# Router logits computed in two halves of 64 tokens, and the value products moved directly behind the next tile's scores

## The chip, the cores and the metric

The kernel runs on one NeuronCore of a Trainium2 chip. The metric is the device time of one execution in microseconds (us). A core has a matrix engine (TensorE; PE in the profile, its weight loads apart as PEld) and engines for elementwise work: VectorE (DVE), ScalarE (ACT) and GpSimd (POOL). SyncE (SP) issues most of the DMA transfers. Each engine takes its instructions in the order of the program, and the engines wait for each other by semaphores.

## The reference

Three layers in a row, cut to what matters:

```python
scores = (q @ k.T) / sqrt(64)                 # 4 batches, 8 heads, 576 positions, head size 64
scores = where((rel >= 0) & (rel < 64), scores, -1e9)   # causal window of 64 keys
attn   = exp(scores - max); attn /= attn.sum() + 1e-9
x      = (attn @ v)                           # as 2304 tokens x 512
noisy  = x @ w_gate + log1p(exp(x @ w_noise)) * noise   # router logits, 8 experts
# the top 2 experts of each token, softmax of their logits
x      = sum over the 2 experts of w * (relu(x @ w1[e]) @ w2[e])
out    = gate(x @ moe2_w_in) @ moe2_w_out     # dense feed-forward layer, hidden size 2048
```

## The kernel before, in words

The 2304 tokens are cut into 18 tiles of 128. The first 104 us are attention and routing, in which this change lies; then come the experts and the dense layer, about 845 us in which TensorE multiplies nearly without a pause.

The attention part is written out by hand as a loop over half-tile **steps** `u` (`step`, L676): a tile has an even step and an odd step. Each engine's queue has the order in which this code calls its parts:

- `A` (L347), in an even step: scores of the next tile. First four products that put the mask into two PSUM banks (L355, 64 rows by 64 columns of the array each), then 16 score products (L364) of the same shape. One bank holds the even heads of the tile, which are scores `u+2`, the other the odd heads, scores `u+3`. Three banks take turns, so the second bank that `A` writes is the one in which the even heads of the tile before stood.
- `Ex` (L418), in an even step: four transposes (L422) of an earlier tile's attention output; ScalarE copies the result to `xt` (L424).
- `C` (L383), in every step: four transposes (L387) of the softmax of one half; ScalarE copies them to `pt` (L389).
- `top` (L368) takes the row maxima on VectorE (L371) and their scaled negative on GpSimd (L373); `soft` (L376) is four exponentials on ScalarE (L380). `soft(u+2)` is called in step `u`.
- `Dm` (L392), at the end of an even step: 16 products with the values (L401, 128 rows by 64 columns of the array), and then the normalization on VectorE (L406, L407, L409) and the store of the tile.
- `Gm` (L435), in an odd step: the router logits of a tile whose `xt` is ready: four products of 128 by 128 (L440), copied out by VectorE (L443).
- `place` (L628): products that count tokens into slots (L634), from step 26 on; `advance` (L636): the routing's work on VectorE in small portions, and its products at L558 to L562.

`Ex`, `C` and `Gm` write two PSUM banks (`bank[3]`, `bank[5]`) in turn (`rot`, L335): within one tile `Ex` has the first, the even `C` the second, the odd `C` the first again, the logits the second. So the odd `C` can start when ScalarE has copied `xt` out. ScalarE's order in a tile is `xt`, even `pt`, exponentials of `u+2`, odd `pt`, exponentials of `u+3`; in every other tile two halves of a weight's conversion (L158) stand behind the exponentials.

Of the kernel before, what the change touches and what calls it, by code (L numbers as in the profile page):

```python
# [26 lines left out]
E, F = 8, 1024  # L27
# [30 lines left out]
def fused_kernel(ctx, tc, qT, kT, v, wg, noise, wcat, out, wd=None):  # L58
    nc = tc.nc
# [41 lines left out]
    def load_qk(j):  # L101
        q_t[j] = qbuf[:, j % 2]
        kt = k_t[j] = qk.tile([P, 4, 320], F32, tag="k", name=f"k{j}")

        for h in (slice(0, P), slice(P, 256)) if j == 0 else (slice(0, 256),):
            t = slice(256 * j + h.start, 256 * j + h.stop)
            nc.sync.dma_start(out=kt[:, :, 64 + h.start:64 + h.stop], in_=kTv[:, :, t])
            nc.sync.dma_start(out=q_t[j][:, :, h], in_=qTv[:, :, t])
        if j == 0:
            nc.vector.memset(kt[:, :, 0:64], 0.0)  # L110


    def keys_before(j):
        nc.gpsimd.tensor_copy(k_t[j][:, :, 0:64], k_t[j - 1][:, :, 256:320])
# [4 lines left out]
    def load_v(i):  # L119
        a = vp.tile([P, H * VW], F32, tag="vE", name=f"vE{i}")  # L120
        nc.sync.dma_start(out=a, in_=v[P * i:P * i + P, :])
        if i == 0:
            vO[0] = vp.tile([P, H * VW], F32, tag="vE", name="vE_")
            nc.vector.memset(vO[0][64:128, :], 0.0)
            nc.sync.dma_start(out=vO[0][0:64, :], in_=v[0:64, :])
        vE[i] = a
# [6 lines left out]
    def load_raw(n, eng=nc.sync):  # L133
        raws[n] = t = raw.tile([P, 1024], F32, tag="raw", name=f"raw{n}")
        if NF <= n < N2:

            if n % NF == 0:
                r = E - 2 if n >= NCE else (n // NF - 1) % (E - 2)
                dyn[n // NF] = nc.values_load(cnt_i[0:1, 1 + r:2 + r], engines=[mybir.EngineType.SP], min_val=0,
                                          max_val=(E - 1) * NF)  # L140
            eng.dma_start(out=t, in_=wcat[bass.ds(dyn[n // NF] + n % NF, 1)].rearrange("o p n -> (o p) n"))
        else:
            eng.dma_start(out=t, in_=wcat[n])
# [114 lines left out]
    wg_sb = ac.tile([P, 4, 32], F32, name="wg_sb")  # L258
# [76 lines left out]
    def rot(u):  # L335
        turn[0] += 1
        return bank[3 + 2 * (turn[0] % 2)] if u <= NU else bank[6]
# [9 lines left out]
    def A(i):  # L347
        j = i // 2
        qo, ko = (i % 2) * P, (i % 2) * P
        sb = [score(2 * i + k) for k in range(2)]  # L350
        for k in range(2):
            r = slice(64 * k, 64 * k + 64)
            for c in range(2):
                m = masks[c][int((2 * i + c) % 9 == 0)]
                nc.tensor.matmul(sb[k][64 * c:64 * c + 64, :], lhsT=id64[r, :],  # L355
                                 rhs=m[r].unsqueeze(1).to_broadcast([64, 4, P]), start=True, stop=False)
        for g in range(4):
            for c in range(2):
                for k in range(2):
                    r = slice(64 * k, 64 * k + 64)  # L360
                    keys = k_t[j][r, g, ko + 64 * c:ko + 64 * c + P]
                    if c == 0:
                        keys = keys.rearrange("p (s n) -> p s n", s=2)[:, ::-1, :]
                    nc.tensor.matmul(sb[k][64 * c:64 * c + 64, g * P:g * P + P],  # L364
                                     lhsT=q_t[j][r, g, qo + 64 * c:qo + 64 * c + 64],
                                     rhs=keys, start=False, stop=(g == 3))
# [9 lines left out]
    def soft(u):  # L376
        sb, nb = score(u), mxs.pop(u)
        p = wk.tile([P, 4, P], F32, tag="p", name=f"p{u}", bufs=4)
        for g in range(4):
            nc.scalar.activation(p[:, g, :], sb[:, g * P:g * P + P], AF.Exp, bias=nb[:, g:g + 1], scale=0.125)  # L380
        pr[u] = p

    def C(u):  # L383
        p = pr.pop(u)
        PTb = rot(u)
        for g in range(4):
            nc.tensor.transpose(PTb[:, g * P:g * P + P], p[:, g, :], idn)  # L387
        t = wk.tile([P, 512], F32, tag="pt", name=f"pt{u}", bufs=PTB)
        nc.scalar.activation(t, PTb, AF.Copy)  # L389
        pts[u] = t  # L390

    def Dm(u):  # L392
        i, r = divmod(u, 2)
        if r == 0:
            return
        ts = [pts.pop(2 * i + k) for k in range(2)]
        for h in range(H):
            g, k = divmod(h, 2)
            for c in range(2):
                vv = (vO, vE)[c][i]  # L400
                nc.tensor.matmul(OB[64 * c:64 * c + 64, h // 4, (h % 4) * VW:(h % 4) * VW + VW],  # L401
                                 lhsT=ts[k][:, g * P + 64 * c:g * P + 64 * c + 64], rhs=vv[:, h * VW:h * VW + VW],
                                 start=True, stop=True)
        ov = OB[:, :, 0:4 * VW].rearrange("p b (h d) -> p b h d", d=VW)
        rl = wk.tile([P, 2, 4, 1], F32, tag="rl", name=f"rl{i}")
        nc.vector.tensor_scalar(out=rl, in0=ov[:, :, :, D:VW], scalar1=1e-9, scalar2=None, op0=ALU.add)  # L406
        nc.vector.reciprocal(out=rl, in_=rl)  # L407
        x = wk.tile([P, H, D], F32, tag="x", name=f"x{i}", bufs=3)
        nc.vector.tensor_tensor(out=x.rearrange("p (b h) d -> p b h d", b=2), in0=ov[:, :, :, 0:D],  # L409
                                in1=rl.to_broadcast([P, 2, 4, D]), op=ALU.mult)  # L410
        xs[i] = x
        nc.sync.dma_start(out=x_dram[P * i:P * i + P, :], in_=x.rearrange("p h d -> p (h d)"))
        if i + 1 < NT:
            if i + 2 < NT:
                nc.gpsimd.tensor_copy(vE[i][0:64, :], vE[i + 1][0:64, :])
            vO[i + 1] = vE[i]
# [18 lines left out]
    def Gm(i, u):  # L435
        g, t = tile_group[i]
        xt = xts.pop(i)
        lg = (rot(u) if u <= NU else bank[0])[:, LGO:LGO + 2 * E]
        for k in range(4):
            nc.tensor.matmul(lg, lhsT=xt[:, k, :], rhs=wg_sb[:, k, 0:2 * E], start=(k == 0), stop=(k == 3))  # L440
        if t == 0:
            lgs_g[g] = gp.tile([P, max(GROUPS), 2 * E], F32, tag="lgs", name=f"lgs{g}", bufs=3)
        nc.vector.tensor_copy(lgs_g[g][:, t, :], lg)  # L443
# [184 lines left out]
    def place():  # L628
        while pq:
            c, o, ej = pq.popleft()  # L630
            if nids[0] == n_early:
                open_ids()
            nids[0] += 1
            nc.tensor.matmul(IDS2[:, c, :], lhsT=o, rhs=ej, start=False, stop=(nids[0] in (n_early, 2 * NT)))  # L634
# [23 lines left out]
    def open_ids():  # L658
        nc.tensor.matmul(IDS[:, 0:2 * NK], lhsT=wz[:, 0:P], rhs=wz[:, 0:2 * NK], start=True, stop=False)
# [16 lines left out]
    def step(u):  # L676
        for c in range(EW):
            if u == L0 + LS * c:
                load_raw(c)
        if u + 2 < NU:  # L680
            if (u + 2) % 4 == 0 and (u + 2) // 4 + 1 < NT // 2:
                load_qk((u + 2) // 4 + 1)
                keys_before((u + 2) // 4 + 1)
            if (u + 1) % 2 == 0 and (u + 1) // 2 + 1 < NT:
                load_v((u + 1) // 2 + 1)


        m = u // 2
        if u % 2 == 0:
            if u + 2 < NU:  # L690
                A(m + 1)
            if u == NU:
                nc.scalar.activation(vE[NT - 2][0:64, :], vE[NT - 1][0:64, :], AF.Copy)
            if u == NU - 2:
                C(u)
            if 0 <= m - 2 < NT:
                Ex(m - 2, u)
        if u < NU and u != NU - 2:
            C(u)
        if u % 2 == 0 and u + 2 < NU:  # L700
            top(u + 2)
            top(u + 3)
        if u + 2 < NU:
            soft(u + 2)

        if u % 2 == 1 and 0 <= m - 2 < NT:
            logits(m - 2, u)
        place()
        early()
        advance(MARKS[u > NU - 10])  # L710
        if 0 <= u - 1 < NU:
            Dm(u - 1)

        for c in range(EW):
            for h in range(2):
                if u == L0 + LS * c + 3 + h:
                    split_w(c, h)
                if u == L0 + LS * c + 4 + h and c < EW - 2:
                    rest_w(c, slice(512 * h, 512 * h + 512))
            if u == L0 + LS * c + 4 and EW <= c + 2 < NF:  # L720
                load_raw(c + 2)
# [291 lines left out]
    t0 = 0  # L1013
# [402 lines left out]
    for q, (ui, p) in enumerate(items):  # L1416
# [5 lines left out]
        while ndone < len(items) and ndone <= q + (1 if items[ndone][0] == FIRST2 else 2):  # L1422
            i = items[ndone]
# [84 lines left out]
```

## Time and profile before

| | |
|---|---|
| time, median of 3 runs | 947.45 us (947.38 to 947.93) |
| the profiled execution | 950.02 us, its span 948.3 us |
| busy over the span | PE 935.7 us (99%), DVE 665.6 (70%), ACT 436.5 (46%), POOL 186.2 (20%) |
| granted TensorE clock | 1.0 in the whole span |

A busy share over the whole span says little of the first tenth of it, which has limits of its own, so the rows below are read from that part. In a timeline a row merges instructions of one line that follow each other: start, time from the first's start to the last's end, engine, line, what is written from what, how many, and in brackets how long the engine stood idle before and what released it. A product of 32-bit numbers shows as two records, so 16 products are x32. Matmuls are pipelined: the ends that are shown overlap the next starts, so costs are read from start to start.

### The profile page before, as it was taken

To read this page: it belongs to the slowest core of one execution; us is meant where nothing else is said; L and a number is where in the kernel's file an instruction comes from. 1 tells how busy PE (TensorE), PEld (TensorE's weight loads), DVE (VectorE), ACT (ScalarE), POOL (GpSimd) and SP (SyncE) were. 2 spreads that over 40 slices of the span, in tenths; PEclk is the share of its full clock that TensorE was granted. 3 is DMA by queue.
4 is the path that set the end of the run, shared out by engine and by line. 5 is a ranking of instruction groups with operands and counts; after the bars stand their busy time and mean duration, and the time that the engine had idled before them with its cause. 6 is when DMAs were issued, how large, how long until landed. Compare 5 with 4: busy or idle time off the path is not lost. (4 is left out here: it accounts for less than half of the span.)

```text
span 948.3 us, 17990 instructions
## 1 busy us (share of the span) xinstructions
PE 935.7 (99%) x6779; PEld 832.3 (88%) x6781; DVE 665.6 (70%) x1411; ACT 436.5 (46%) x907; POOL 186.2 (20%) x249
## 2 busy tenths in 40 slices
PE   9999999999999999999999999999999999999998
PEld 6887888988888989898888889988999899899986
DVE  4689765477997968889533366767867776687664
ACT  6898314345565555555433266333433333342221
POOL 3222013133645353354402030000000000000000
PEclk9999999999999999999999999999999999999999
DMA  8874136555888878767725566775576559556521
GB/s 258 300 252 167 56 100 186 188 191 199 290 288 275 261 236 277 257 206 260 252 89 184 204 231 236 252 256 178 177 256 213 164 174 308 175 178 213 182 95 44
DMA packets 91274, 196.95 MB, mean 208 GB/s; under 512 B 7320, under 2 KB 18072, under 8 KB 91184
## 3 DMA queue, kind: packets, MB, share of 16 engines
q1 hardware_dynamic: 83152, 171.68, 54.6%
q0 software_dynamic: 6736, 21.86, 6.4%
q10 hardware_dynamic: 1296, 2.23, 0.6%
q8 instruction: 54, 0.88, 0.4%
q14 instruction: 36, 0.29, 0.1%
HBM read 155.45 MB, written 40.29 MB: 206 GB/s over the span
## 5 line engine op out<-in xcount | busy, mean ns | idle before, releaser
L969 PE MATMUL bank<-wo,hall 128*128 128x512 f32 x864 | 237.6, 394 | 0.0
L969 PE MATMUL bank<-w,hall 128*128 128x512 f32 (+3 forms) x944 | 234.6, 396 | 0.1
L969 PEld LDWEIGHTS bank<-w,hall 128*128 128x128 f32 (+3 forms) x944 | 167.7, 183 | 35.2 <-issue 0.3
L969 PEld LDWEIGHTS bank<-wo,hall 128*128 128x128 f32 x864 | 146.7, 188 | 17.4 <-DVE hall L915 0.2
L904 ACT ACTIVATE hall<-bank 128x288 fp32r<-128x288 f32 (+6 forms) x128 | 54.0, 422 | 218.4 <-PE bank L896 200.6
L896 PE MATMUL bank<-xhie,w 128*128 128x288 f32 (+4 forms) x768 | 122.5, 302 | 0.3 <-DVE hall L907 0.2
L896 PEld LDWEIGHTS bank<-xhie,w 128*128 128x128 f32 x768 | 113.5, 188 | 7.1 <-DVE hall L907 1.4
L907 DVE SCALAR_TENSOR_TENSOR hall<-bank,hall 128x288 fp32r<-128x288 f32 (+7 forms) x168 | 60.0, 391 | 82.5 <-ACT hall L904 75.1
L149 DVE TENSOR_TENSOR w<-raw,w 128x1024 fp32r<-128x1024 f32 (+1 forms) x69 | 81.9, 1188 | 23.8 <-ACT w L158 17.8
L1183 PEld LDWEIGHTS bank<-xb,wi 128*128 128x128 f32 x576 | 80.8, 188 | 8.4 <-DVE cg L1173 0.7
L1207 ACT ACTIVATE hall<-cg 128x512 fp32r<-128x512 f32 x64 | 40.3, 629 | 100.4 <-DVE cg L1205 100.4
L1183 PE MATMUL bank<-xb,wi 128*128 128x256 f32 x576 | 84.3, 282 | 0.3 <-DVE cg L1173 0.3
L1183 PEld LDWEIGHTS bank<-xc,wi 128*128 128x128 f32 x480 | 67.5, 188 | 6.5
L1183 PE MATMUL bank<-xc,wi 128*128 128x256 f32 x480 | 69.9, 280 | 0.0
L158 ACT ACTIVATE w<-raw 128x1024 fp32r<-128x1024 f32 (+1 forms) x71 | 69.4, 977 | 0.0
L896 PE MATMUL bank<-xloe,w 128*128 128x288 f32 (+4 forms) x384 | 69.0, 301 | 0.0
L1201 ACT ACTIVATE mg<-cg 128x512 f32<-128x512 f32 x64 | 40.1, 626 | 45.8 <-DVE cg L1173 44.1
L204 POOL TENSOR_TENSOR td<-rawd 128x512 f32<-128x512 f32 x32 | 33.3, 1040 | 139.6 <-DVE rawd L202 111.8
L896 PEld LDWEIGHTS bank<-xloe,w 128*128 128x128 f32 x384 | 58.0, 188 | 0.0
L1202 DVE SCALAR_TENSOR_TENSOR cg<-mg,cg 128x512 f32<-128x512 f32 x64 | 43.8, 684 | 18.8 <-ACT mg L1201 18.8
L1211 DVE SCALAR_TENSOR_TENSOR hall<-cg,hall 128x512 fp32r<-128x512 f32 x64 | 44.0, 687 | 8.1 <-ACT hall L1207 7.7
L1205 DVE SCALAR_TENSOR_TENSOR cg<-mg,cg 128x512 f32<-128x512 f32 x64 | 44.0, 687 | 1.0
(285 smaller groups left out, 1389.2 us busy)
## 6 DMA issues: line engine op xcount, KB each, us to landing
wi<-w1o SPq DMA_DIRECT2D x56, 1024.0 KB
raw<-wcat SPq DMA_DIRECT2D x64, 512.0 KB
rawd<-wd SPq DMA_DIRECT2D x32, 512.0 KB
w1o<-so SPq DMA_DIRECT2D x64, 256.0 KB
y<-y_dram SPq DMA_DIRECT2D x28, 256.0 KB
vE<-v SPq DMA_DIRECT2D x18, 260.0 KB
x_dram<-x SPq DMA_DIRECT2D x18, 256.0 KB
k<-kT SPq DMA_DIRECT2D x8, 512.0 KB
```

Of the source, the lines that this page charges most:

```text
L149: nc.vector.tensor_tensor(out=w[:, 1, c], in0=t[:, c], in1=w[:, 0, c].bitcast(F32), op=ALU.subtract)
L158: nc.scalar.activation(w[:, 0, c], t[:, c], AF.Copy)
L896: nc.tensor.matmul(ps, lhsT=l[k], rhs=r[:, k, s:s + w], start=(c == 0), stop=(c == len(prods) - 1))
L904: nc.scalar.activation(hh, ps, AF.Relu)
L907: nc.vector.scalar_tensor_tensor(out=t, in0=ps[:, c], scalar=0.0, in1=hh[:, c].bitcast(F32), op0=ALU.max, op1=ALU.subtract)
L969: nc.tensor.matmul(M2[b][0:w], lhsT=h2[:, o:o + w], rhs=r[n], start=(first and a == 0), stop=(last and a == end))
L1183: nc.tensor.matmul(ps, lhsT=w[:, l, k * P:k * P + P], rhs=r[:, m, k, :], start=(c == 0), stop=(c == len(prods) - 1))
L1201: nc.scalar.activation(st["m"], c, AF.Relu, scale=0.5)
L1202: nc.vector.scalar_tensor_tensor(out=c, in0=st["m"], scalar=1.0, in1=c, op0=ALU.min, op1=ALU.subtract)
L1205: nc.vector.scalar_tensor_tensor(out=c, in0=st["m"], scalar=1.0, in1=c, op0=ALU.min, op1=ALU.mult)
L1207: nc.scalar.activation(h2[:, 0:T], c, AF.Copy, scale=-1.0)
L1211: nc.vector.scalar_tensor_tensor(out=h2[:, T:2 * T], in0=c, scalar=-1.0, in1=h2[:, 0:T].bitcast(F32), op0=ALU.mult, op1=ALU.subtract)
```

## The change

Three edits. The router logits are computed by halves of 64 tokens: eight products of 128 rows by 64 columns of the array instead of four of 128 by 128, alternating between the two halves. `place` is called ahead of the logits instead of behind them. `Dm` keeps only its products and is called directly behind `A`, from step 4 on; the normalization becomes `norm` and is called where `Dm` was.

```diff
+    def norm(u):
+        i, r = divmod(u, 2)
+        if r == 0:
+            return
         ov = OB[:, :, 0:4 * VW].rearrange("p b (h d) -> p b h d", d=VW)
...
         for k in range(4):
-            nc.tensor.matmul(lg, lhsT=xt[:, k, :], rhs=wg_sb[:, k, 0:2 * E], start=(k == 0), stop=(k == 3))
+            for t0 in (0, 64):
+                s = slice(t0, t0 + 64)
+                nc.tensor.matmul(lg[s], lhsT=xt[:, k, s], rhs=wg_sb[:, k, 0:2 * E], start=(k == 0), stop=(k == 3))
...
                 A(m + 1)
             if u == NU:
                 nc.scalar.activation(vE[NT - 2][0:64, :], vE[NT - 1][0:64, :], AF.Copy)
+            if u > 2:
+                Dm(u - 1)
...
+        place()
         if u % 2 == 1 and 0 <= m - 2 < NT:
             logits(m - 2, u)
-        place()
         early()
         advance(MARKS[u > NU - 10])
         if 0 <= u - 1 < NU:
-            Dm(u - 1)
+            if u <= 2:
+                Dm(u - 1)
+            norm(u - 1)
```

TensorE's queue in one tile, steps 12 and 13, before. `k3` and `qbuf` are keys and queries, `x4` a tile's attention output, `p12` and `p13` the softmax halves, `pt10` and `pt11` the transposed ones of the tile before, `vE4` and `vE5` values, `ob` the bank of the value products:

```order
L364 MATMUL bank0_73<-k3_487,qbuf_109 64x128
L422 MATMUL bank5_77<-idn_164,x4_738 128x128 [waits DVE_49,Activation_49]
L387 MATMUL bank3_76<-idn_164,p12_714 128x128 [waits DVE_49]
L401 MATMUL ob_106<-vE4_466,pt10_704 64x65 [waits Pool_49]
L401 MATMUL ob_106<-vE5_560,pt10_704 64x65 [waits DMAHW7_49]
L401 MATMUL ob_106<-vE4_466,pt11_749 64x65
...
L387 MATMUL bank5_77<-idn_164,p13_751 128x128 [waits Activation_49]
L440 MATMUL bank3_76<-wg_sb_128,xt4_785 128x16 [waits Activation_49]
L355 MATMUL bank1_74<-mask00_134,id64_132 64x512
L355 MATMUL bank2_75<-mask00_134,id64_132 64x512 [waits Activation_49]
```

The same tile in the changed kernel (L427 is L422 of before, L447 is L440):

```order
L364 MATMUL bank0_73<-k3_491,qbuf_109 64x128
L401 MATMUL ob_106<-vE4_466,pt10_732 64x65 [waits DVE_49,Pool_49]
L401 MATMUL ob_106<-vE5_564,pt10_732 64x65 [waits DMAHW7_49]
L401 MATMUL ob_106<-vE4_466,pt11_761 64x65 [waits Activation_49]
...
L427 MATMUL bank5_77<-idn_164,x4_750 128x128 x4
L387 MATMUL bank3_76<-idn_164,p12_742 128x128 [waits DVE_49]
L387 MATMUL bank5_77<-idn_164,p13_763 128x128 [waits Activation_49]
L447 MATMUL bank3_76<-wg_sb_128,xt4_817 64x16 [waits Activation_49]
L447 MATMUL bank3_76<-wg_sb_128,xt4_817 64x16 x7
L355 MATMUL bank1_74<-mask00_134,id64_132 64x512
L355 MATMUL bank2_75<-mask00_134,id64_132 64x512 [waits Activation_49]
```

The 16 value products moved from between the two sets of softmax transposes (L387) to between the scores and the transposes of `x`. The second bank's masks wait for ScalarE in both. ScalarE's, VectorE's and GpSimd's queues hold the same instructions in the same order in both kernels.

TensorE's queue in step 27, where `place` runs, before (`ohr`, `ohe` are a token's marks, `bank7` the slots):

```order
L387 MATMUL bank3_76<-idn_164,p27_1437 128x128 x3
L440 MATMUL bank5_77<-wg_sb_128,xt11_1506 128x16 [waits Activation_49]
L440 MATMUL bank5_77<-wg_sb_128,xt11_1506 128x16 x3
L634 LDWEIGHTS ohr0_1_0_1529 [waits DVE_49]
L634 MATMUL bank7_78<-ohe0_1_0_1531,ohr0_1_0_1529 128x145 [waits DVE_49]
```

And in the changed kernel (L641 is L634 of before):

```order
L387 MATMUL bank3_76<-idn_164,p27_1477 128x128 x3
L641 LDWEIGHTS ohr0_1_0_1589 [waits DVE_49]
L641 MATMUL bank7_78<-ohe0_1_0_1591,ohr0_1_0_1589 128x145 [waits DVE_49]
L641 LDWEIGHTS ohr0_1_1_1593 [waits DVE_49]
L641 MATMUL bank7_78<-ohe0_1_1_1595,ohr0_1_1_1593 128x145 [waits DVE_49]
L447 MATMUL bank5_77<-wg_sb_128,xt11_1566 64x16 [waits Activation_49]
L447 MATMUL bank5_77<-wg_sb_128,xt11_1566 64x16 x7
```

The logits now stand behind two products that wait for marks which VectorE makes.

## Rows read from the trace of the kernel before

**Rows 1.** Busy by stretch: window, length, PE, PEld, DVE, ACT, POOL (count), clock, DMA.
```profile
32.00:42.00 10.00, 10.00 (x199) 8.98 (x200) 6.52 (x15) 9.01 (x27) 2.63 (x9) 1.00 0.85 287
72.00:82.00 10.00, 9.43 (x155) 7.78 (x154) 9.76 (x51) 9.96 (x31) 1.49 (x4) 1.00 0.74 262
92.00:102.00 10.00, 8.21 (x113) 7.06 (x112) 5.56 (x23) 4.31 (x9) 3.16 (x3) 1.00 0.51 160
```
**Rows 2.** Timeline of TensorE's products, one tile of the attention stage.
```profile
24.88 0.41 PE L355 MATMUL bank<-mask,id 64*64 64x512 bf16 x4
...
26.10 0.66 PE L422 MATMUL bank<-idn,x 128*128 128x128 f32 x4
26.59 0.60 PE L387 MATMUL bank<-idn,p 128*128 128x128 f32 x4
27.12 1.15 PE L401 MATMUL ob<-vE,pt 128*64 128x65 f32 x32
28.20 0.65 PE L387 MATMUL bank<-idn,p 128*128 128x128 f32 x4
28.70 0.96 PE L440 MATMUL bank<-wg_sb,xt 128*128 128x16 f32 x8
29.59 0.41 PE L355 MATMUL bank<-mask,id 64*64 64x512 bf16 x4
```
**Rows 3.** Timeline of TensorE's weight loads in the same tile.
```profile
26.09 0.42 PEld L422 LDWEIGHTS bank<-idn,x 128*128 128x128 f32 x4 [0.17 <-ACT p L380]
...
27.12 1.01 PEld L401 LDWEIGHTS ob<-vE,pt 128*64 128x64 f32 x32 [0.17 <-issue]
...
28.59 0.97 PEld L440 LDWEIGHTS bank<-wg_sb,xt 128*128 128x128 f32 x8
```
**Rows 4.** Timeline of ScalarE in the same tile.
```profile
26.79 0.60 ACT L424 ACTIVATE xt<-bank 128x512 f32<-128x512 f32 x1 [0.91 <-PE bank L422]
27.29 0.59 ACT L389 ACTIVATE pt<-bank 128x512 f32<-128x512 f32 x1
27.76 1.15 ACT L380 ACTIVATE p<-bank,nb 128x128 f32<-128x128 f32 x4
28.76 0.66 ACT L158 ACTIVATE w<-raw 128x512 fp32r<-128x512 f32 x1
29.28 0.63 ACT L389 ACTIVATE pt<-bank 128x512 f32<-128x512 f32 x1
```
**Rows 5.** TensorE in step 2, where the masks waited for ScalarE.
```profile
11.88 0.40 PE L355 MATMUL bank<-mask,id 64*64 64x512 bf16 x2 [0.85 <-ACT p L380]
...
13.08 0.66 PE L387 MATMUL bank<-idn,p 128*128 128x128 f32 x4
```
**Rows 6.** TensorE's masks of step 4 and of step 24, ten tiles on.
```profile
15.34 0.54 PE L355 MATMUL bank<-mask,id 64*64 64x512 bf16 x4
...
62.60 0.41 PE L355 MATMUL bank<-mask,id 64*64 64x512 bf16 x4
```
**Rows 7.** Timeline of steps 24 to 26: the routing's first products.
```profile
63.81 0.66 PE L422 MATMUL bank<-idn,x 128*128 128x128 f32 x4
...
66.99 0.63 ACT L389 ACTIVATE pt<-bank 128x512 f32<-128x512 f32 x1
...
67.67 0.19 PE L558 MATMUL bank<-ohs,tri 128*128 128x64 bf16 x1 [0.30 <-ACT pt L389]
...
67.98 0.41 PE L355 MATMUL bank<-mask,id 64*64 64x512 bf16 x4
...
68.22 1.04 PE L364 MATMUL bank<-k,qbuf 64*64 64x128 f32 x32
...
69.89 1.28 DVE L371 TENSOR_REDUCE mx<-bank 128x4 f32<-128x512 f32 x2
```
**Rows 8.** VectorE in steps 26 and 27: the last marks, the logits' copy.
```profile
71.73 0.70 DVE L593 TENSOR_SCALAR ohe<-io,rf 128x145 f16<-128x145 f16 x1
...
73.37 0.16 DVE L443 COPY lgs<-bank 128x16 f32<-128x16 f32 x1
```

## The prediction, made before the changed kernel was run

> **What bounds the kernel now.** The page's table by slices gives the place first: all that the diff touches runs in the first tenth of the span, and behind it TensorE is at 9 tenths or more in nearly every slice, so a microsecond won or lost in the attention part goes one to one into the time. Second, the busy times by stretch [rows 1]: in 32 to 42 us TensorE has no idle time (10.00), ScalarE is at 9.01 and VectorE at 6.52; in 72 to 82 us VectorE is at 9.76 and ScalarE at 9.96 of 10, with TensorE at 9.43. So there are two stages. Up to about 62 us TensorE sets the pace, with ScalarE close behind; from there to 92 us it is VectorE, which then does the routing as well. Third, the timeline of TensorE for one tile [rows 2]: from one set of masks to the next are 29.59 - 24.88 = 4.71 us: masks and scores 1.22 (24.88 to 26.10), transposes of `x` 0.49, even softmax transposes 0.53, value products 1.08, odd transposes 0.50, logits 0.89. Last, ScalarE in that tile [rows 4]: `xt` starts 0.69 behind the first transpose of `x` (26.79 against 26.10) after 0.91 us of idle time, then `pt`, then four exponentials that end at 27.76 + 1.15 = 28.91. ScalarE does wait for TensorE, but TensorE hardly for ScalarE: the masks at 29.59 come 0.68 behind the exponentials that must have freed their second bank. That 0.68 is all the slack there is.
>
> **The logits by halves.** Four products of 128x128 become eight of 128x64. The trace has this shape in the value products: 16 of them take 1.08 us [rows 2], so eight take 0.54, the two changes of the array's shape around them included. That is 0.35 less than the 0.89 of now, per tile, on TensorE.
>
> The Trainium skill ("TensorE: Matmul & The Clock Gate", The mechanism) says that a weight load overlaps running products only where it goes to other rows of the array; both halves use all 128 rows, so by that rule the halves would gain nothing. The trace disagrees: 32 loads of 64 columns took 1.01 us, 32 ns each, against 121 ns for a load of 128 columns in the logits (0.97 for 8) [rows 3]. One half after the other, at half of 121 each, they would have taken 1.9.
>
> **The value products behind the scores.** The same 16 products, so 1.08 us again on TensorE. What changes is what stands between the transposes of `x` and the masks of the next tile, and so who waits. With E for the first transpose of `x`, in us from E:
>
> - The even softmax transposes come at 0.49, as before. The odd ones came at 2.10 (28.20 - 26.10) and could now come at about 0.9. But they write the bank from which ScalarE copies `xt`, which ends at 0.69 + 0.60 = 1.29; with 0.05 from ScalarE's end to TensorE's start (66.99 + 0.63 = 67.62, and 67.67, [rows 7]) they start at 1.34. The value products had covered this; now about 0.4 us of waiting takes their place.
> - Odd transposes 0.50 and logits 0.54 take TensorE to the next masks at about 2.4. The second bank's masks must wait for the even exponentials: `xt` 0.69, 0.50 on to `pt`, 0.47 on to the exponentials, 1.15 for them [rows 4], 0.05 to TensorE: 2.86. TensorE waits here another 0.4 or so.
> - From these masks to what follows the scores are 1.20: in step 2 the masks were released so, at 11.88, and the transposes behind the scores started at 13.08 [rows 5]. There the value products now stand, 1.08, and then the next tile's transposes of `x`.
>
> So a loop closes: 2.86 + 1.20 + 1.08 = 5.14 us per tile. Before, the same loop was without the 1.08, 4.06, and hidden under TensorE's 4.71. The value products have moved from beside ScalarE's work into a chain with it: ScalarE idles while TensorE does scores, values and the transposes of `x`, and TensorE idles while ScalarE does `xt`, `pt` and the exponentials. What the halves save lies in front of the second wait and is swallowed by it. In tiles with weight conversion a second loop runs over the odd `pt` (in rows 4 it starts at 29.28, ends at 29.91, which is E + 3.81); the value products need it at about E + 4.1, so it is not the longer one.
>
> I take 5.14, though the shape changes from 64x64 to 128x64 behind the scores, which the trace does not show. Two other changes of shape show 0.17 of idle time of the weight loads, into the transposes of `x` and into the value products [rows 3]; the 1.20 has the first of them in it. Without it the loop is 4.97. On the other side, a wait more of that size makes 5.31.
>
> The Trainium skill ("TensorEngine Tiling (Array Packing)", Key Properties) states that a change of the tiling mode drains TensorE, of the tile within a mode not. Each tile has four changes of mode before and four after; by that rule nothing is saved, which speaks for 5.14 and against 4.97, and no run here shows this change yet.
>
> **The sum.** The ten tiles from 15.34 to 62.60 take 47.26 us [rows 6], 4.73 each; at 5.14 they take 51.4: +4.1. In the next tile the routing's products wait for the odd `pt` (67.62), and the masks come at 67.98, E + 4.17 with E at 63.81 [rows 7]. With 1.20 and 1.08 behind it the tile takes 6.45, against 67.98 - 62.60 = 5.38: +1.1, of which VectorE takes up 0.5, since its maxima at 69.89 came that much behind the scores' end (68.22 + 1.04 = 69.26, and about 0.1 on the way to VectorE, an estimate): +0.6. Then VectorE sets the pace: its work is the same, and TensorE's loop of 5.14 fits into its tiles. One thing is added: the logits now stand behind `place`, and `place` behind VectorE's marks, while VectorE's next steps are the normalization and then the copy of those logits. The marks ended at 72.43, the copy started at 73.37, 0.94 on [rows 8]. Placing, the logits' 0.54 and the way through take about that long: 0 to 0.4 per tile in two tiles that place in an odd step, I take +0.3 in all. In the last 10 us the transposes of the last tiles wait for their `x` and ScalarE for them; the order gains and loses cover in turn, with TensorE at 8.21 of 10 [rows 1]: 0, with 0.5 to either side. The normalization where it was costs nothing new: its products end earlier, and `x` is needed two tiles later. Sum: 4.1 + 0.6 + 0.3 = +5.0. Against the profiled execution's 950.02 that is 955.0; it lies 2.57 above the median of the runs, so for the median I forecast 947.45 + 5.0 = 952.4. Its own range: with 4.97 the ten tiles cost 2.4 and the step with routing 0.3, with nothing else 950.1; with 5.31 and 0.5 at the end 954.8.
>
> **The rivals.**
>
> - *The halves are paid for and the wait is not there: faster.* If TensorE's own work set the pace on, each of the ten tiles would lose 0.35: -3.5, 943.9. For it: TensorE has no idle time in this stage now. Against it: the loop. It turns at the point where ScalarE's part falls from 2.86 to 4.71 - 1.20 - 1.08 = 2.43; all five of its pieces are read from rows and none of them is touched by the change.
> - *No drain behind the scores: no change, or almost.* The loop is 4.97 or less, if the scores and the values flow into each other and the change out of the values is shorter too. At 4.9 the ten tiles cost 1.7, VectorE's slack of 0.5 in step 26 takes part of it and the halves give a little back in the last tiles: 947.45 + 1.3 = 948.8. For it: the shape of the columns, 64, is the same in both, so this would be an easier change than those in the rows. Against it: the 0.17 shows wherever the weight loads can be seen to change.
> - *The halves do not run beside each other: slower still.* Then the logits take 16 loads of half of 121 ns, 0.97 and two changes of shape, about 1.2: the masks come at 3.1 instead of 2.86, the loop is 5.4 and the ten tiles cost 6.7: 947.45 + 6.7 + 0.9 = 955.0. Against it speak the loads of the value products [rows 3].
>
> **Chances.** My forecast 0.58, the halves one after the other 0.09, no drain 0.20, faster 0.13. A measurement of this kernel can tell 0.2%, 1.9 us, from no change: slower begins at 949.4, faster ends at 945.5. The forecast and the serial halves are slower throughout, 0.67, and of the drainless case 0.05 goes there: 0.72 slower. The rest of that case, with 0.02 of the faster one that comes out small, is 0.17 within; 0.11 faster. The range from 947.6 to 955.2 leaves out the faster case and little more.
>
> **What will show it.** In the profile of the changed kernel: the distance from masks to masks in 20 to 60 us, 5.1 where it was 4.7; TensorE idle in front of the second masks, released by the exponentials, and in front of the odd transposes, released by `xt`, some 0.4 us each per tile; `xt` on ScalarE with over 0.9 us of idle time in every tile, in front of it, where it was in every other; the logits at half a microsecond. Attention should end about 5 us later and the rest keep its length. I am wrong if the distance stays at 4.7 or below, if the masks do not wait, or if the clock is granted at less than 1.0 in this stage because TensorE now pauses in it; in 92 to 102 us it paused more, and the row shows 1.00 [rows 1].

## The result, and the profile after

The changed kernel takes 955.38 us (median of 6 runs, 953.39 to 956.37); the kernel before, run beside it, 947.94 (947.38 to 948.96). The ratio is 1.0078, 95% interval 1.0067 to 1.0088: 7.4 us slower, where +5.0 and at most 955.2 had been forecast. Two of the six runs, at a mean granted clock of 1.00, took 953.39 and 953.93; the four at 0.996 to 0.998 took 955.11 to 956.37.

One tile of the attention stage on TensorE, after (timeline: start, length, engine, line, what, count, idle time before), to be read against [rows 2]:

```profile
35.05 0.76 PE L355 MATMUL bank<-mask,id 64*64 64x512 bf16 x4
35.42 1.27 PE L364 MATMUL bank<-k,qbuf 64*64 64x128 f32 x32
36.62 1.15 PE L401 MATMUL ob<-vE,pt 128*64 128x65 f32 x32
37.70 0.66 PE L427 MATMUL bank<-idn,x 128*128 128x128 f32 x4
...
39.05 0.66 PE L387 MATMUL bank<-idn,p 128*128 128x128 f32 x4 [0.25 <-ACT xt L429]
39.63 0.65 PE L447 MATMUL bank<-wg_sb,xt 128*64 128x16 f32 x16
40.21 0.76 PE L355 MATMUL bank<-mask,id 64*64 64x512 bf16 x4
```

From masks to masks are 40.21 - 35.05 = 5.16 us; before they were 4.71. Both waits of the loop are there: the odd transposes behind `xt`, and the row of masks, 0.76 where it was 0.41, because its second half waits. The logits take 40.21 - 39.63 = 0.58. ScalarE in the same tile, after, which answers to [rows 4]:

```profile
38.40 0.60 ACT L429 ACTIVATE xt<-bank 128x512 f32<-128x512 f32 x1 [1.51 <-PE bank L427]
38.89 0.59 ACT L389 ACTIVATE pt<-bank 128x512 f32<-128x512 f32 x1
39.37 1.15 ACT L380 ACTIVATE p<-bank,nb 128x128 f32<-128x128 f32 x4
```

The exponentials end at 39.37 + 1.15 = 40.52, so the second masks can start about 0.35 behind the first at 40.21. Before `xt` ScalarE now idles 1.51 or 0.47 us by turns. The ends of the stage, after, which answer to [rows 6], and the first product of the experts, 103.73 before:

```profile
14.65 0.54 PE L355 MATMUL bank<-mask,id 64*64 64x512 bf16 x4
...
65.97 0.76 PE L355 MATMUL bank<-mask,id 64*64 64x512 bf16 x4
...
111.50 1.66 PE L907 MATMUL bank<-xhi0a,w 128*128 128x384 f32 x8
```

The ten tiles take 51.32 us, +4.06. Steps 24 to 26, after, which answer to [rows 7] (TensorE, ScalarE and VectorE together):

```profile
71.81 0.63 ACT L389 ACTIVATE pt<-bank 128x512 f32<-128x512 f32 x1
72.49 0.21 PE L565 MATMUL bank<-ohs,tri 128*128 128x64 bf16 x1 [1.29 <-ACT pt L389]
...
72.89 0.64 PE L355 MATMUL bank<-mask,id 64*64 64x512 bf16 x4
...
73.07 0.29 DVE L574 TENSOR_TENSOR o<-o,bank 128x128 f32<-128x128 f32 x1 [1.48 <-PE bank L569]
73.32 1.92 PE L364 MATMUL bank<-k,qbuf 64*64 64x128 f32 x32
...
75.37 1.29 DVE L371 TENSOR_REDUCE mx<-bank 128x4 f32<-128x512 f32 x2 [0.48 <-PE bank L364]
```

This tile takes 72.89 - 65.97 = 6.92, +1.54. TensorE pauses 1.29 us for the odd `pt`, VectorE waits 1.48 us for the routing's products, and then the scores take 1.92 us where they took 1.04. The busy time by stretch, after (length, PE, PEld, DVE, ACT, POOL, granted clock, DMA), shows why; the first three rows answer to [rows 1]:

```profile
32.00:42.00 10.00, 9.50 (x189) 7.65 (x186) 5.85 (x15) 8.01 (x24) 2.34 (x7) 1.00 0.78 259
72.00:82.00 10.00, 9.39 (x180) 8.04 (x180) 7.78 (x29) 7.33 (x23) 1.21 (x4) 0.83 0.94 311
82.00:92.00 10.00, 8.75 (x127) 7.15 (x125) 9.17 (x47) 7.34 (x21) 1.89 (x6) 0.83 0.21 63
...
70.00:72.00 2.00, 1.20 (x20) 1.02 (x21) 1.48 (x6) 2.00 (x7) 0.22 (x1) 1.00 0.03 11
72.00:74.00 2.00, 1.51 (x29) 1.30 (x32) 0.83 (x4) 1.48 (x5) 0.00 (x0) 0.58 0.81 205
74.00:76.00 2.00, 2.00 (x44) 1.67 (x38) 1.52 (x8) 1.24 (x3) 0.00 (x0) 0.56 0.96 327
...
86.00:88.00 2.00, 2.00 (x39) 1.74 (x36) 1.82 (x18) 2.00 (x8) 0.00 (x0) 0.50 0.66 171
```

Behind the pause of 1.29 us, and again behind one of 1.17 in front of `place` (84.83), TensorE's clock is granted at about half, 1.2 instead of 2.4 GHz. Steps 26 to the experts take 111.50 - 72.89 = 38.61 us; before 103.73 - 67.98 = 35.75. Scores and values at half clock account for 2.5 of these 2.86: from start to start the scores take 1.85 instead of 0.97 twice, and the values 1.33 and 1.58 instead of 1.08.

The differences add up to more than the medians show: 4.06 + 1.54 + 2.86 = 8.5, less 0.7 by which the masks of step 4 came earlier in this execution. The profiled execution of before had a wait of 2.2 us near 154 us (transposes of gathered rows) that its median runs, over 2 us shorter, probably did not have: in later sets of runs this wait stood in the profile of every kernel of two sets, where the kernel before took 950.5 and 951.0, and of none in the two others, where it took 948.0 and 947.8. So times are compared within a set only.

### The profile page after: what moved, and what is told of

Its sections match the earlier page's. It is cut to its first block, busy times and chain, and to the rows that moved or that the text cites. A ratio compares the mean times of both kernels' runs of the same rounds, so it can differ in the third digit from the quotient of the medians.

```text
span 953.9 us, 18282 instructions
## 1 busy us (share of the span) xinstructions
PE 936.7 (98%) x6923; PEld 829.8 (87%) x6925; DVE 666.4 (70%) x1411; ACT 436.7 (46%) x907; POOL 185.4 (19%) x249
```

## The experiments

Five sets of runs with the one above, each against the kernel before in the same set. "Measured" gives a median in us, that of the kernel before, and the recorded ratio with its 95% interval in brackets; the ratio can differ slightly from the quotient of the two medians.

**The halves alone.** The kernel before with this one edit:

```diff
-            nc.tensor.matmul(lg, lhsT=xt[:, k, :], ...)
+            for t0 in (0, 64):
+                nc.tensor.matmul(lg[t0:t0 + 64], lhsT=xt[:, k, t0:t0 + 64], ...)
```

> The kernel before with the logits by halves alone: the value products and the counting stand where they were. Loop theory (value products behind the scores close a loop through ScalarE; the halves themselves are cheap): no loop over 4.06 us, so TensorE's own work sets the pace and falls by 0.35 us per tile, from 4.71 to about 4.36 from masks to masks; ten tiles give -3.5, VectorE's stage behind them gives some of it back: 944 to 946 us beside 947.9. Rival (the halves cost, one after the other, or by changes of the array's shape): masks to masks 4.7 or above, 948 to 951. Granted clock 1.0 by both.

Measured: 948.05 against 947.97, 1.0005 (0.9992 to 1.0018). A miss for the loop theory's number, and the profile says why. TensorE's waits between 14 and 64 us (engine, line, releaser: total, times, longest):

```profile
PE bank L364 <- DMA qbuf<-qT: 1.9, 2, 1.7
```

and the longer of the two in the timeline of TensorE:

```profile
47.68 0.41 PE L355 MATMUL bank<-mask,id 64*64 64x512 bf16 x4
49.78 1.10 PE L364 MATMUL bank<-k,qbuf 64*64 64x128 f32 x32 [1.69 <-DMA qbuf<-qT]
...
54.08 0.41 PE L355 MATMUL bank<-mask,id 64*64 64x512 bf16 x4
```

The usual tile is 4.48, 0.23 shorter than before, but one took 6.40 and one 4.92: TensorE overtook the loading of the queries, and the ten tiles took 47.30, as long as before.

**The halves, loads issued earlier.**

```diff
-            if (u + 2) % 4 == 0 and (u + 2) // 4 + 1 < NT // 2:
+            if u == 2:
                 load_qk(...)
...
                 A(m + 1)
+                if u > 2 and u % 4 == 0 and u // 4 + 2 < NT // 2:
+                    load_qk(u // 4 + 2)
+                    keys_before(u // 4 + 2)
```

> The kernel before with the logits by halves, and the loads of the next queries and keys issued two steps earlier, straight behind the scores that free their buffers (from step 4 on). With the halves alone the tiles were 4.48 us, but the scores at 29.93 and 49.78 waited 0.21 and 1.69 us for the queries. Theory (the halves do shorten the tile, and the gain was given back to these loads): no such wait, ten tiles in 44.8 to 45.2 instead of 47.3, VectorE's stage takes part of it back: 945.5 to 947. Rival (the transfers themselves are full, so that an earlier issue lands no earlier, or delays the values and weights): the waits stay, 948 or more.

> The halves with the queries' and keys' loads issued earlier, again, on another chip: 0.5 to 2 us below the kernel before, as on the first (ratio 0.9987). If that was an accident of the first chip: level, ratio 0.9995 to 1.001.

Measured: 949.34 against 950.48, 0.9987 (0.9978 to 0.9996); in another set 949.50 against 950.97, 0.9982 (0.9973 to 0.9992). The tile of the first run:

```profile
43.05 0.41 PE L355 MATMUL bank<-mask,id 64*64 64x512 bf16 x4
...
46.37 0.66 PE L387 MATMUL bank<-idn,p 128*128 128x128 f32 x4
46.95 0.65 PE L447 MATMUL bank<-wg_sb,xt 128*64 128x16 f32 x16
47.53 0.41 PE L355 MATMUL bank<-mask,id 64*64 64x512 bf16 x4
```

No tile waits for queries in either profile; in the first the tiles at 20.07 and 25.03 took 4.96 and 4.58, behind exponentials on ScalarE that had waited 0.77 us for GpSimd. The halves do pay: logits 0.58 for 0.89, with 0.58 instead of 0.50 from the odd transposes to them, so 0.23 a tile. The ten tiles take 45.51 and 44.93 us, and the experts start 2.1 and 2.4 us earlier than in the kernel before. This version is the only one that beats the kernel before, by 1.1 and 1.5 us.

**The values alone.** The kernel before with `Dm` behind `A`, and `norm` where it was:

```diff
+            if u > 2:
+                Dm(u - 1)
```

> The kernel before with the value products moved alone: whole logits, counting behind them. Loop theory: the whole logits end at 0.69 + 0.60 + 0.05 + 0.50 + 0.89 = 2.73 us behind the first transpose of x, still ahead of the even exponentials at 2.86, so masks to masks are 5.15 as in the changed kernel, and the time 953 to 956. Rival (the halves are what costs): masks to masks back at 4.7, about 948. Rival (counting ahead of the logits costs): 1 us or more below the changed kernel, with the 5.15 unchanged.

> The value products moved alone, again, beside the changed kernel on the same chip. Theory: +5.5 to +6.5 over the kernel before, 1 to 2 below the changed kernel; what lies between them is the half-speed clock behind the longer pauses that the shorter logits and the counting first leave. Rival (the halves and the counting cost or give nothing): within 0.7 of the changed kernel.

Measured: 954.18 against 947.97, 1.0072 (1.0055 to 1.0089); again 954.20 against 947.77, 1.0067 (1.0052 to 1.0082). One tile:

```profile
31.12 0.44 PE L355 MATMUL bank<-mask,id 64*64 64x512 bf16 x4
...
34.79 0.66 PE L387 MATMUL bank<-idn,p 128*128 128x128 f32 x4 [0.25 <-ACT xt L429]
35.28 1.06 PE L445 MATMUL bank<-wg_sb,xt 128*128 128x16 f32 x8
36.27 0.44 PE L355 MATMUL bank<-mask,id 64*64 64x512 bf16 x4
```

5.15 again, with logits of 0.99: TensorE is 0.32 later at the masks, and these wait 0.03 instead of 0.35. The halves are swallowed whole in the loop. Moving the values alone costs 6.2 and 6.4 us; the changed kernel, in the one set that has both, costs 8.4, so 1.9 us are left for the two other edits and for what the clock does. Steps 24 to 26 took 6.49 and 6.50, with a pause of 0.97. The clock stayed at 1.00 in the first profile and fell to 0.50 behind that pause in the second.

**A shorter loop.** The changed kernel, but in the even steps 4 to 20 (`swap(u)`) VectorE copies `pt`:

```diff
+        if swap(u):
+            top(u + 2)
+            top(u + 3)
         if u < NU and u != NU - 2:
             C(u)
...
+        nc.vector.tensor_copy(t, PTb) if swap(u) else nc.scalar.activation(t, PTb, AF.Copy)
```

> The changed kernel, but in the even steps 4 to 20 the softmax transposes are copied to pt by VectorE, behind the row maxima, instead of by ScalarE. It takes 0.47 us out of the loop through ScalarE (xt, pt, exponentials, masks, scores, values, transposes of x) and leaves TensorE's products as they are. Loop theory: masks to masks 4.7 in those nine tiles instead of 5.15, about -4: 951 to 952. Rival (the moved value products cost TensorE the time itself, by changes of the array's shape): masks to masks stay at 5.15, 955.

Measured: 958.54 against 950.48, 1.0081 (1.0065 to 1.0096). TensorE and ScalarE in one tile:

```profile
38.01 0.60 ACT L432 ACTIVATE xt<-bank 128x512 f32<-128x512 f32 x1 [1.71 <-PE bank L430]
38.50 1.13 ACT L380 ACTIVATE p<-bank,nb 128x128 f32<-128x128 f32 x4
38.66 0.65 PE L390 MATMUL bank<-idn,p 128*128 128x128 f32 x4 [0.31 <-ACT xt L432]
39.24 0.65 PE L450 MATMUL bank<-wg_sb,xt 128*64 128x16 f32 x16
...
39.82 0.41 PE L355 MATMUL bank<-mask,id 64*64 64x512 bf16 x4
```

With the copy off ScalarE the masks wait no longer (0.41), and the tile falls to 4.86 on TensorE's own products and the wait for `xt`. The loop through the exponentials is shown; 0.29 of its 0.47 came back, since the shorter loop over `xt` alone ends last then. The ten tiles took 48.97 us, 2.35 less than in the changed kernel, but the time did not fall with them: the ratio is like the changed kernel's in its sets (1.0078 to 1.0092; it was not run in this one). In this profile the clock was granted at 0.88 and 0.83 in 72 to 82 and 82 to 92 us, much as in the changed kernel, and TensorE waited 1.1 us for loaded rows near 559 us, where the three profiles of the changed kernel show 0.9 or none. What else took the gain stays open.

**Where in the loop's steps.** The changed kernel with `Dm` behind `A` only up to step 22, or only from step 24 (old place otherwise):

```diff
-            if u > 2:
+            if 2 < u < 24:        # the other run: if u >= 24:
                 Dm(u - 1)
```

> The changed kernel, but from step 24 on the value products stand again where they were (halves and counting order as changed). Loop theory: 5.15 from masks to masks up to step 24, +4.1 over the kernel before; the step with the routing's products back near 5.4, VectorE's stage at its old length and TensorE's clock at 1.00 in it: 951 to 952.5. Rival (the stage of the routing, its waits and the clock in it carry the loss): 948 to 949.

> The changed kernel, but up to step 22 the value products stand where they were. Loop theory: masks to masks 4.36 up to step 24 (-3.5 or so), then the step with the routing's products some 1.5 us longer than before, and VectorE's stage longer with a granted clock below 1.0 in it (+1 to +3): 946 to 949. Rival (only the routing stage is dear): 951 or more.

Measured: up to 22, 953.45 against 947.97, 1.0063 (1.0046 to 1.0080), above what was expected; from 24 on, 951.84, 1.0035 (1.0018 to 1.0052), above as well. Up to 22: ten tiles +4.06, the next +0.36, from there to the experts +0.06; the clock fell late, in 97 to 102 us, though TensorE's pauses from 66 us to there were all under 0.6 us, and near 555 us TensorE waited 1.3 us for loaded rows. From 24 on: the ten tiles give only 1.2 (a tile of 5.36 waits for queries), the next tile costs +1.12 and the rest +3.2, with the clock as this window shows:

```profile
68.00:70.00 2.00, 2.00 (x32) 1.53 (x36) 1.71 (x9) 1.11 (x5) 0.00 (x0) 0.50 1.03 294
```

Both stages cost, and neither alone makes the whole loss.

**The counting's place.**

> The kernel before with the halves and the counting ahead of the logits; the value products stand where they were. With the halves alone it was level with the kernel before. Prediction's term for the counting first: +0.3. Theory now (it puts the logits behind the pause in which TensorE waits for the marks, and leaves the pause bare): +0.5 to +2 over the kernel before, with pauses of about 1 us in front of the counting. Rival (it costs nothing while the value products stand between): level, within 0.5.

> The changed kernel with the counting behind the logits again, as it was before (halves and moved value products stay). In the changed kernel TensorE idled 1.17 us in front of a counting product at 84.83, the logits came behind it, and the granted clock fell to about half after it. Theory (loop, then pauses in the routing steps, then the clock): the logits stand in that pause again, masks to masks are 5.15 up to step 24 as before, the clock falls less often: 953.5 to 954.5, near the run with the value products moved alone. Rival (the order of counting and logits costs nothing; the halves keep TensorE waiting): 955 to 956, the clock below 1.0 as often.

Halves with `place` first, values not moved: 947.72 against 947.77, 1.0009 (0.9995 to 1.0023), pauses of 0.2 to 0.6: it costs nothing measurable there. Halves and values with `place` behind the logits: 957.55 against 950.48, 1.0075 (1.0059 to 1.0090): in its profile the clock fell once instead of twice, but the time, 7.1 us above the kernel before, is where the rival put it and is not told from the changed kernel's. The rival is not excluded.

**The pauses filled.** The changed kernel with five products that no one reads (128 by 512, a dead bank) in steps 25, 29 and 33, or 25 and 29 alone; and four in step 25 with the values moved alone:

```diff
+        if u in (29, 33):
+            warm(5, Sb[u % 3])
         place()
...
+        if u == 25:
+            warm(5, Sb[u % 3])
```

> The changed kernel with five idle-filling products of 128 by 512 into a dead bank in each of three pauses of TensorE: behind the logits in step 25, ahead of the counting in steps 29 and 33. They compute nothing that is used. Clock theory (the clock falls because of these pauses, and that is about 2 us): granted clock 1.00 up to 92 us in every run, 953 to 954. Rival (the pauses cost what they last and the clock only shows it): 955 to 957, since the fillers add work.

> The changed kernel unaltered, as the base on the same chip for the other runs of this set. Its ratio to the kernel before should be 1.0078 as it was, +7 to +8 us; its profile should show the granted clock at about half behind the pauses of 1.29 us (in front of the routing's products) and 1.17 us (in front of the counting), as all profiles of kernels with the moved values, the halves and the counting first have.

> The changed kernel with five idle-filling products in each of three pauses, again, now beside the changed kernel on the same chip. In its first profile the clock stayed at 1.00 up to 100 us and attention was 3 us shorter than in the changed kernel's. Clock theory: 1.5 to 3 us below the changed kernel. Rival (what attention gains is lost behind it, in the waits for gathered rows, or the clock falls elsewhere): within 1 us of it.

> The changed kernel unaltered, as the base on this chip: +7.4 to +8.4 us over the kernel before, the clock at about half behind the pauses of 1.29 and 1.17 us.

> The changed kernel with five idle-filling products behind the logits in step 25 and five ahead of the counting in step 29, the two pauses behind which the clock fell; none in step 33. Clock theory: clock 1.00 through attention, and without the long wait for loaded rows near 550 us the time is 1.5 to 2.5 us below the changed kernel's. Rival (the wait near 550 us takes back what attention gains): within 1 us of it, with that wait at 1.8 us or more again.

> The value products moved alone, with four idle-filling products behind the logits in step 25, where TensorE paused 0.97 us and the clock fell in one of two profiles. Clock theory: clock 1.00 in attention in every run, +5.5 to +6.2 over the kernel before, against +6.3 without the fillers. Rival (the clock's fall there costs nothing that shows): +6.3 or more.

Measured: filled 958.13 against 950.48, 1.0085 (1.0070 to 1.0101). Beside each other in one set: changed 956.14, 1.0092 (1.0077 to 1.0107), filled 955.23, 1.0082 (1.0068 to 1.0095), before 947.77. In another: changed 958.72, 1.0083 (1.0064 to 1.0101), filled in two steps 957.68, 1.0067 (1.0050 to 1.0084), values alone and filled 958.32, 1.0067 (1.0049 to 1.0084), before 950.97. The first filled profile by stretch:

```profile
72.00:74.00 2.00, 1.89 (x52) 1.45 (x52) 1.13 (x7) 1.26 (x5) 0.00 (x0) 1.00 0.62 174
...
86.00:88.00 2.00, 2.00 (x40) 1.78 (x34) 2.00 (x8) 1.26 (x4) 0.22 (x1) 1.00 0.54 141
```

and its masks of step 26 and first product of the experts in the timeline:

```profile
72.59 0.41 PE L355 MATMUL bank<-mask,id 64*64 64x512 bf16 x4
...
108.50 1.66 PE L911 MATMUL bank<-xhi0a,w 128*128 128x384 f32 x8
```

From step 26 to the experts 108.50 - 72.59 = 35.91 us, as in the kernel before; without the fillers 38.61, and 38.76 in its second profile. In the third profile of the changed kernel the pauses stand unaltered in the timeline of TensorE:

```profile
73.39 0.19 PE L565 MATMUL bank<-ohs,tri 128*128 128x64 bf16 x1 [1.29 <-ACT pt L389]
73.70 0.41 PE L355 MATMUL bank<-mask,id 64*64 64x512 bf16 x4
...
84.36 0.65 PE L641 MATMUL bank<-ohe,ohr 128*128 128x145 f16 x4 [1.17 <-ACT ohe L603]
```

and the clock did not fall behind them, as the stretches behind either pause show:

```profile
74.00:76.00 2.00, 2.00 (x69) 1.76 (x61) 1.90 (x10) 1.14 (x5) 0.00 (x0) 1.00 0.89 260
...
86.00:88.00 2.00, 2.00 (x66) 1.76 (x59) 2.00 (x18) 1.77 (x6) 0.00 (x0) 1.00 0.75 246
```

There the experts start at 109.46, 35.76 behind the masks of step 26: with the same instructions, the half-speed clock is the whole difference between 35.8 and 38.7. So its price in attention, 2.3 to 3 us, is shown (38.61 and 38.76 against 35.76, 35.91 and, in the second filled profile, 36.26). In the time it is shown by less. The fillers gained 0.9 and 1.0 us, with intervals that overlap the changed kernel's, where 1.5 to 3 and 1.5 to 2.5 had been expected; and the values alone with fillers lie 7.4 us above the kernel before (1.0067 by the ratio, 6.4 us), where the clock theory had 5.5 to 6.2. Both profiles of the three fillers have a wait for loaded rows near 550 us of

```profile
PE bank L776 <- POOL y L1065: 1.8, 1, 1.8
```

1.8 us (the other 1.9), against 0.9 in one profile of the changed kernel and none in two; and with two fillers, where that wait is not, the clock fell at 98 to 102 us, behind the third pause. So the rival holds in part: some of what the clock returns is lost further on, and why the rows come later there stays open. The clock also falls behind attention. In the third profile of the changed kernel, which kept 1.00 in attention, it fell behind the wait of 2.2 us for gathered rows:

```profile
160.00:170.00 10.00, 10.00 (x59) 8.93 (x58) 6.86 (x10) 5.35 (x9) 0.00 (x0) 0.83 0.48 138
```

This execution took 7.1 us more than the median of the kernel before in its set, against the 5.5 of its attention. The profile of the values alone with fillers shows the same fall at 160 us.

## Why the prediction came out too low

- **The loop: right, in mechanism and size.** 5.16 instead of 5.14 per tile, +4.06 instead of +4.1, both waits in their places; with the copy off ScalarE the wait of the masks is gone. By the rule that a change of the tiling mode drains the array (Trainium skill, "TensorEngine Tiling (Array Packing)", Key Properties) it was to be 5.14 and not 4.97; the trace's 5.16 agrees.
- **The halves: right in the loop, mis-sized outside.** They were to be swallowed, and up to step 26 the values alone cost as much: from the masks of step 4 to those of step 26 are 58.09 us with them, and 58.09 in the third profile of the changed kernel. The rival "the halves are paid for" priced them at 0.35 a tile and 943.9 in all: it is 0.23, and without earlier loads nothing. The rule by which a weight load overlaps running products only on other rows (Trainium skill, "TensorE: Matmul & The Clock Gate", The mechanism), as the prediction read it, would give no gain; the 0.58 for 0.89 disagrees.
- **The step with the routing's products: the first step that failed.** It said that of +1.1 "VectorE takes up 0.5, since its maxima at 69.89 came that much behind the scores' end". The tile grew by 1.54 (1.43 in the third profile), and nothing was taken up. VectorE in the kernel before, from what reads the routing's products on to the maxima of [rows 7]:

```profile
68.16 0.29 DVE L567 TENSOR_TENSOR o<-o,bank 128x128 f32<-128x128 f32 x1
...
69.43 0.54 DVE L586 TENSOR_SCALAR ohr<-io,rf,tcode 128x128 f16<-128x128 f16 x2
```

  And in the third profile of the changed kernel (L574 is L567 of before):

```profile
73.88 0.29 DVE L574 TENSOR_TENSOR o<-o,bank 128x128 f32<-128x128 f32 x1 [1.39 <-PE bank L569]
...
75.61 1.28 DVE L371 TENSOR_REDUCE mx<-bank 128x4 f32<-128x512 f32 x2
```

  What lay between scores and maxima was not slack but this work, which reads the routing's products (L567 reads their bank). From its start to the maxima are 69.89 - 68.16 = 1.73 us before and 75.61 - 73.88 = 1.73 after: late products move it and the maxima alike, and VectorE idles 1.39 us (1.48 in the first profile) in front of it. The tile's own length was near: 6.45 forecast, 6.50 with whole logits, 6.8 to 6.9 with the halves, which reach the first masks 0.35 sooner.
- **VectorE's stage: +0.3 forecast, 0.0 at full clock** (35.76 against 35.75 in the third profile), **+2.9 at half clock: the step that failed by most.** The +0.3 for the logits behind the counting did not show at all. The prediction named the clock as what would make it wrong, but argued it away from 92 to 102 us, where TensorE was less busy and the clock 1.00, and gave it no term and no place in the range. That row adds up several short pauses; the longest in it is

```profile
96.73 0.63 PE L422 MATMUL bank<-idn,x 128*128 128x128 f32 x4 [0.65 <-ACT pt L389]
```

  while the change makes TensorE pause 1.29 and 1.17 us in one piece. In the loop's own stage, where the prediction put its two new waits, the clock stayed at 1.00 as forecast.
- **The sum.** At full clock 4.02 + 1.43 + 0.01 = +5.5 in the third profile's attention; the two runs at a clock of 1.00 are 5.7 above the kernel before, and at 953.4 and 953.9 still inside the forecast range. The four at a lower clock lie 955.7 - 953.7 = 2.0 higher on average, and these carry the median out of it. That the clock makes all of these 2.0 is not shown, since the fillers gave back about 1. Forecast and result differ by 0.8 to 0.9 in the one step, less 0.3 in the other, and by the clock. That the +0.3 which did not come hid a part of the step's error is luck.

## What to carry to other kernels

An interval between two events on another engine is slack only if what fills it does not hang on the thing that comes late; follow what that engine does in it before it is counted as cover. When a change makes TensorE wait in one piece, price the half-speed clock as a case of its own, with the products behind the pause at twice their length. A tile made shorter moves the demand for its loads: check when the next buffer lands before the gain is counted.

## What the runs showed that had not been expected

- The clock's fall is not settled by the pause alone. With the pauses of 1.29 and 1.17 us it fell behind the first in two of three profiles of the changed kernel, and in the three other kernels that had the 1.29; with 0.97 in one of two; with 0.3 to 0.6 in step 25 in none of the six with the values not moved there; with the pause filled in none of four. Pauses under 0.6 us did not keep it up everywhere (the values moved up to step 22: 0.50 in 98 to 100 us), and behind the wait of 2.1 to 2.2 us for gathered rows near 154 us it fell in three of the nine profiles that have this wait.
- A mean clock of 0.996 to 0.998 over the span, which looks like nothing, went with 1.5 to 2.7 us in the first runs of the changed kernel.
- The kernel before took 947.8 to 951.0 us from set to set, with one wait of 2.1 to 2.2 us for gathered rows present or absent in all profiles of a set.
